# Attention with a gated second branch: the input loaded first, layernorm in groups, and the second branch cut into stages inside the attention loop

**Chip, cores, metric.** One core of a Trainium2 chip. Times are device microseconds (us) of one execution, medians over the runs named. TensorE is PE, VectorE DVE, ScalarE ACT, GpSimd POOL in the profile; L12 is line 12 of the kernel that is spoken of.

## The reference, cut

```python
xn = layernorm(x)                                  # x: 2048 x 640
s  = attention(xn, k_cache, v_cache, wq, wo)       # branch A: 32 heads of 192, last 512 keys
# branch B: a router picks 2 tokens, which get a gated MLP (1536 wide)
r   = xn @ w_r;  idx = argsort(-r)[:2]
y   = (silu(xn[idx] @ w_gate) * (xn[idx] @ w_up)) @ w_down * sigmoid(r[idx])
g   = silu(xn + scatter_add(y at idx))
out = x + s * g
```

Only the last line joins the branches. B's result g is needed at the very end, xn at the very start.

## The kernel before

Attention runs over 16 pairs of heads, four query blocks of 512 rows each: `kT_ps` (keys transposed, once a pair), `q_ps` (query projection), `s_ps` (scores, 8 row tiles a block), softmax on DVE and ACT, `pT_ps` (transposed probabilities), `o_ps`; after each two pairs an output projection (`y_ps`, 192 matmuls) is added into `acc`. A scheduler orders the instructions within each engine; a PE instruction that isn't ready holds up all behind it (here PE stood idle for 9.88 us ahead of the selb matmul of branch B, with attention's work behind it).

```python
loaded = {0: load_pair(0)}                 # 16 loads on the SyncE queue, ahead of x
for t in range(NT):                        # NT = 16 tiles of 128 rows
    eng = nc.sync if t % 2 == 0 else nc.gpsimd
    eng.dma_start(out=x_all[:, t, :], ...)
    ... bn_stats, bn_aggr -> mv_all[:, t]
rstd_all = ...                             # one step for all 16 tiles
for t in range(NT):
    nc.vector.tensor_scalar(out=xn_all[:, t, :], in0=x_all[:, t, :], ...)   # L140
    for d0 in range(0, DT, 4):             # 4 blocks, then 1: two PSUM tiles, two copies
        pst = ps_a.tile(...)               # ps_a has two buffers
        ... nc.tensor.transpose(pst[:, dt, :], ...)                         # L146
        nc.any.tensor_copy(out=xnT[...], in_=pst[...])                      # L147
# branch B in one piece, bs pool with 3 buffers for its weights
r_ps (L162) -> r_row -> r_bf -> r_rt -> max (L170) -> max_index (L172) -> selb -> E
xs_ps (L211, 80 matmuls) -> h: 24 loads w_c, 120 matmuls y_ps (L223) -> down (L241) -> gate g (L249, L251)
... then: for pi in range(NPAIR): attention
```

Of the kernel before, what the change touches and what calls it, by code (L numbers as in the profile page):

```python
# [8 lines left out]
ACT = mybir.ActivationFunctionType  # L9
ALU = mybir.AluOpType  # L10
AX = mybir.AxisListType
F32 = mybir.dt.float32  # L12
BF16 = mybir.dt.bfloat16
# [6 lines left out]
def kernel(  # L20
# [97 lines left out]
    loaded = {0: load_pair(0)}  # L118

    with tc.tile_pool(name="ln", bufs=1) as lnp, tc.tile_pool(name="lns", bufs=4) as lns:  # L120
        FMAX = nc.vector.BN_STATS_FMAX
        nch = (D + FMAX - 1) // FMAX
        while D % nch != 0:
            nch += 1
        csz = D // nch
        x_all = lnp.tile([P, NT, D], BF16, name="x_all")
        mv_all = lnp.tile([P, NT, nc.vector.BN_AGGR_DIM], F32, name="mv_all")
        for t in range(NT):
            eng = nc.sync if t % 2 == 0 else nc.gpsimd
            eng.dma_start(out=x_all[:, t, :], in_=x2[t * P:(t + 1) * P, :])  # L130
            stats = lns.tile([P, nch, nc.vector.BN_STATS_DIM], F32, name="stats")
            for c in range(nch):
                nc.vector.bn_stats(out=stats[:, c, :], in_=x_all[:, t, c * csz:(c + 1) * csz])  # L133
            nc.vector.bn_aggr(out=mv_all[:, t, :], in_=stats[:])
        rstd_all = lnp.tile([P, NT], F32, name="rstd_all")
        nc.vector.tensor_scalar_add(out=rstd_all[:], in0=mv_all[:, :, 1], scalar1=EPS)
        nc.scalar.activation(out=rstd_all[:], in_=rstd_all[:], func=ACT.Sqrt)
        nc.vector.reciprocal(out=rstd_all[:], in_=rstd_all[:])
        for t in range(NT):
            nc.vector.tensor_scalar(out=xn_all[:, t, :], in0=x_all[:, t, :], scalar1=mv_all[:, t, 0:1],  # L140
                                    scalar2=rstd_all[:, t:t + 1], op0=ALU.subtract, op1=ALU.mult)
# [7 lines left out]
    with tc.tile_pool(name="bw", bufs=1) as bw, tc.tile_pool(name="bs", bufs=3) as bs:  # L149
# [3 lines left out]
        wg_v = B_w_gate.rearrange("(dt p) f -> p dt f", p=P)  # L153
        wu_v = B_w_up.rearrange("(dt p) f -> p dt f", p=P)

        r_row = bw.tile([1, S], F32, name="r_row", tag="rowA")
        RC = 512
        for c0 in range(0, S, RC):
# [5 lines left out]
            nc.vector.tensor_copy(out=r_row[:, c0:c0 + cw], in_=r_ps[:, :cw])  # L164
        r_bf = bw.tile([1, S], BF16, name="r_bf")
        nc.vector.tensor_copy(out=r_bf[:], in_=r_row[:])
        r_rt = bw.tile([1, S], F32, name="r_rt", tag="rowB")
        nc.vector.tensor_copy(out=r_rt[:], in_=r_bf[:])
        mx8 = bw.tile([1, 8], F32, name="mx8")
        nc.vector.max(out=mx8[:], in_=r_rt[:])  # L170
        idx8 = bw.tile([1, 8], U32, name="idx8")
        nc.vector.max_index(out=idx8[:], in_max=mx8[:], in_values=r_rt[:])  # L172
        sel = bw.tile([1, 4], F32, name="sel")
        nc.vector.tensor_copy(out=sel[:, 0:2], in_=idx8[:, 0:2])
        nc.vector.tensor_copy(out=sel[:, 2:4], in_=mx8[:, 0:2])
# [10 lines left out]
        sig = bw.tile([2, 1], F32, name="sig")  # L186
        nc.scalar.activation(out=sig[:], in_=selT[:, 1:2], func=ACT.Exp, scale=-1.0)
        nc.vector.tensor_scalar_add(out=sig[:], in0=sig[:], scalar1=1.0)
        nc.vector.reciprocal(out=sig[:], in_=sig[:])

        iota_tok_i = bw.tile([P, NT], I32, name="iota_tok_i")
        nc.gpsimd.iota(iota_tok_i[:], pattern=[[P, NT]], base=0, channel_multiplier=1)
        iota_tok = bw.tile([P, NT], F32, name="iota_tok")
        nc.vector.tensor_copy(out=iota_tok[:], in_=iota_tok_i[:])
        E = bw.tile([P, NT, 2], BF16, name="E")
        for j in range(2):
            nc.vector.tensor_scalar(out=E[:, :, j], in0=iota_tok[:], scalar1=selb[:, j:j + 1],
                                    scalar2=None, op0=ALU.is_equal)
        iota_row_i = bw.tile([2, S], I32, name="iota_row_i", tag="rowA")
        nc.gpsimd.iota(iota_row_i[:], pattern=[[1, S]], base=0, channel_multiplier=0)  # L200
        iota_row = bw.tile([2, S], F32, name="iota_row", tag="rowB")
        nc.vector.tensor_copy(out=iota_row[:], in_=iota_row_i[:])
        ET = bw.tile([2, S], BF16, name="ET")
        nc.vector.tensor_scalar(out=ET[:], in0=iota_row[:], scalar1=selT[:, 0:1], scalar2=0.5,
                                op0=ALU.is_equal, op1=ALU.mult)

        xselT = bw.tile([P, DT, 2], BF16, name="xselT")
        xs_ps = ps_a.tile([P, DT, 2], F32, name="xs_ps", tag="ps_a")
        for dt in range(DT):
            for c in range(NT):  # L210
                nc.tensor.matmul(xs_ps[:, dt, :], lhsT=xn_all[:, c, dt * P:(dt + 1) * P], rhs=E[:, c, :],  # L211
                                 start=(c == 0), stop=(c == NT - 1))
        nc.vector.tensor_copy(out=xselT[:], in_=xs_ps[:])

        h_ps2 = ps_y.tile([P, 2, 512], F32, name="y_ps2")
        hg_ps = h_ps2[:, 0, :2 * FT].rearrange("p (f j) -> p f j", j=2)
        hu_ps = h_ps2[:, 1, :2 * FT].rearrange("p (f j) -> p f j", j=2)
        for (w_v, h_ps, eng) in ((wg_v, hg_ps, nc.gpsimd), (wu_v, hu_ps, nc.gpsimd)):
            for ft in range(FT):
                w_c = bs.tile([P, DT, P], BF16, name="w_c", tag="bs")  # L220
                eng.dma_start(out=w_c[:], in_=w_v[:, :, ft * P:(ft + 1) * P])
# [176 lines left out]
```

## Time and profile before

| | us |
|---|---|
| median of the first 5 runs | 1164.95 (1163.77 to 1170.2) |
| span of the profiled run | 1166.7 |
| PE busy | 1088.5 (93%) |
| first `kT_ps` / first `s_ps` (here and below the second matmul of the first pair; the first starts 0.2 earlier) | 69.7 / 78.4 |

The prediction below shows the totals, the stages and the chain of the head. The pace of the transposes, from the timeline (start, us, instruction, in brackets the idle time before it and who ended it):

```profile
34.08 0.69 PE L146 MATMUL pst<-ident,xn_all 128*128 128x128 bf16 x5 [0.57 <-ACT xnT L147]
34.71 0.75 ACT L147 COPY xnT<-pst 128x512 bf16<-128x512 bf16 x2 [0.51 <-PE pst L146]
35.34 0.69 PE L146 MATMUL pst<-ident,xn_all 128*128 128x128 bf16 x5 [0.57 <-ACT xnT L147]
```

PE and ACT take turns: a tile needs both PSUM buffers, so PE waits for ACT's copies before the next tile, 1.26 us a tile. What B's weight tile w_c made the engines wait for (us, times):

```profile
  DMA w_c<-in_B_w_up_dram: 8.6, 15
  DMA w_c<-in_B_w_gate_dram: 3.7, 9
```

### The profile page before, as it was taken

What the parts mean: (1) busy time and instruction counts of PE and PEld (TensorE: products, weight loads), DVE (VectorE), ACT (ScalarE), POOL (GpSimd) and SP (SyncE); (2) the same over time, 40 slices, a digit from 0 to 9 for tenths busy, and PEclk for the clock granted to TensorE, in tenths of its full rate; (3) what the DMA queues carried; (4) which work ended last, traced back from release to release, by engine and by line L of the source; (5) the groups of instructions that cost most, each with busy time, mean ns of one, the idle gap of its engine ahead of it and who ended that gap; (6) DMA issues with size and microseconds to landing.
All of it is one profiled execution on the core that took longest, in us unless ns stands there. A gap on an engine that the chain in (4) does not pass through costs nothing.

```text
span 1166.7 us, 19485 instructions
## 1 busy us (share of the span) xinstructions
PE 1088.5 (93%) x7178; PEld 589.2 (51%) x7178; DVE 896.9 (77%) x2206; ACT 735.4 (63%) x1701; POOL 52.2 (4%) x85
## 2 busy tenths in 40 slices
PE   0568999999999999999999999999999999999996
PEld 0334445654456545654456445654456545654553
DVE  4567889668966989578966989578966989578995
ACT  0336778457854878458754878468754878468651
POOL 3044000000000000000000000000000000000000
PEclk9979999999999999999999999999999999999997
DMA  9034110111020200112020100112020100010121
GB/s 228 1 76 125 31 32 19 28 35 36 11 45 21 45 14 18 28 35 40 7 45 26 40 15 18 28 35 41 5 44 27 40 15 17 15 35 1 41 63 62
DMA packets 125119, 43.33 MB, mean 37 GB/s; under 512 B 111968, under 2 KB 123232, under 8 KB 125024
## 3 DMA queue, kind: packets, MB, share of 16 engines
q1 hardware_dynamic: 122496, 34.88, 13.5%
q0 software_dynamic: 2528, 7.21, 2.1%
q8 instruction: 56, 0.92, 0.3%
q14 instruction: 39, 0.32, 0.1%
HBM read 39.45 MB, written 2.62 MB: 36 GB/s over the span
## 4 chain that ended last, share of the span: by engine, by line
PE 75%; DVE 9%; ACT 8%; issue 3%; DMA 2%; SPq 1%; POOL 0%; ACTq 0%; POOLq 0%
PE o_ps L345 18%; PE y_ps L269 16%; PE q_ps L310 13%; PE pT_ps L338 9%; PE s_ps L324 9%; PE s_ps L325 7%; ACT p_sb L330 5%; DVE nmx L327 2%; ACT oT_p L347 2%; DVE acc L277 1%; ACT pT L340 1%; DVE stats L133 1%; DMA w_c<-in_B_w_up_dram 1%; DVE diag L335 1%; DMA wd_c<-in_B_w_down_dram 1%
## 5 line engine op out<-in xcount | busy, mean ns | idle before, releaser
L330 ACT ACTIVATE p_sb<-s_ps,nmx 128x512 bf16<-128x512 f32 x512 | 352.1, 690 | 101.4 <-DVE nmx L327 77.0
L327 DVE TENSOR_REDUCE nmx<-s_ps 128x1 f32<-128x512 f32 x512 | 347.4, 684 | 32.7 <-PE s_ps L325 25.1
L310 PE MATMUL q_ps<-xnT,wq_p 128*128 128x512 bf16 x960 | 284.0, 381 | 0.6 <-ACT kT_p L300 0.6
L345 PE MATMUL o_ps<-pT,v_p 128*128 128x512 bf16 x1024 | 263.9, 379 | 3.3 <-ACT oT_p L347 0.7
L269 PE MATMUL y_ps<-wo_p,oT_p 128*128 128x320 bf16 x1536 | 247.8, 302 | 4.6 <-DVE acc L277 3.9
L340 ACT CAST pT<-pT_ps 128x512 bf16<-128x512 f32 x312 | 182.3, 584 | 90.7 <-PE pT_ps L338 87.8
L338 PEld LDWEIGHTS <-p_sb 128*128 128x128 bf16 x2048 | 151.8, 97 | 131.5 <-issue 23.3
L338 PE MATMUL pT_ps<-diag,p_sb 128*128 128x128 bf16 x2048 | 199.9, 219 | 5.8 <-DVE diag L335 4.0
L324 PE MATMUL s_ps<-kT_p,qT_p 128*128 128x512 bf16 x512 | 193.5, 378 | 5.0 <-ACT p_sb L330 1.3
L325 PE MATMUL s_ps<-kT_p,qT_p 128*128 128x512 bf16 x512 | 193.7, 378 | 0.0
L269 PEld LDWEIGHTS <-oT_p 128*128 128x128 bf16 x1536 | 148.9, 99 | 82.7 <-issue 6.4
L277 DVE TENSOR_TENSOR acc<-acc,y_ps 128x640 f32<-128x640 f32 x112 | 91.7, 819 | 107.0 <-PE y_ps L269 106.2
L345 PEld LDWEIGHTS <-v_p 128*128 128x128 bf16 x1024 | 98.2, 97 | 128.0 <-issue 33.5
L347 ACT CAST oT_p<-o_ps 128x512 bf16<-128x512 f32 (+1 forms) x164 | 95.6, 583 | 102.6 <-PE o_ps L345 102.1
L340 DVE CAST pT<-pT_ps 128x512 bf16<-128x512 f32 x200 | 137.8, 689 | 20.6 <-PE pT_ps L338 14.9
L335 DVE TENSOR_SCALAR diag<-ident,rr 128x128 bf16<-128x128 bf16 x512 | 131.7, 257 | 8.0
L310 PEld LDWEIGHTS <-wq_p 128*128 128x128 bf16 x960 | 89.1, 98 | 70.9 <-issue 2.7
L315 ACT ACTIVATE qT_p<-q_ps 128x512 bf16<-128x512 f32 x128 | 76.7, 599 | 53.1 <-PE q_ps L310 53.0
L330 ACT ACTIVATION_READ_ACCUMULATOR p_sb<-s_ps,nmx 128x1 f32 x512 | 102.7, 201 | 0.0
L333 DVE RECIPROCAL rr<-rs 128x1 f32<-128x1 f32 x512 | 80.3, 157 | 25.3 <-ACT p_sb L330 21.1
L325 PEld LDWEIGHTS <-qT_p 128*128 128x128 bf16 x512 | 49.6, 97 | 47.8 <-issue 25.3
L347 DVE CAST oT_p<-o_ps 64x512 bf16<-64x512 f32 (+1 forms) x92 | 63.4, 689 | 11.7 <-PE o_ps L345 11.4
(82 smaller groups left out, 407.5 us busy)
## 6 DMA issues: line engine op xcount, KB each, us to landing
wq_p<-in_A_wq_dram SPq DMA_DIRECT2D x32, 160.0 KB, 2.8
wo_p<-in_A_wo_dram SPq DMA_DIRECT2D x32, 160.0 KB, 2.5
k_p<-in_A_k_cache_dram SPq DMA_DIRECT2D x32, 128.0 KB, 2.4
v_p<-in_A_v_cache_dram SPq DMA_DIRECT2D x32, 128.0 KB, 2.5
wq_p<-in_A_wq_dram SPq DMA_DIRECT2D x32, 80.0 KB, 2.8
wo_p<-in_A_wo_dram SPq DMA_DIRECT2D x32, 80.0 KB, 2.4
x_f<-in_A_x_dram SPq DMA_DIRECT2D x16, 160.0 KB, 2.3
out_dram<-o_t SPq DMA_DIRECT2D x16, 160.0 KB, 1.8
```

Source lines behind the costliest of these rows:

```text
L269: nc.tensor.matmul(y_ps2[:, nh, :NH], lhsT=oT_g[:, b, ts_], rhs=wo_g[:, b, nh * NH:(nh + 1) * NH], start=(i == 0), stop=(i == nmm - 1))
L277: nc.vector.tensor_tensor(out=acc_v, in0=acc_v, in1=y_ps2[:, :, :NH], op=ALU.add)
L310: nc.tensor.matmul(q_ps[:], lhsT=wq_p[:, dt, b, :], rhs=xnT[:, dt, q0:q0 + QC], start=(dt == 0), stop=(dt == DT - 1))
L324: nc.tensor.matmul(s_ps[:], lhsT=qT_p[:, bq, qs], rhs=kT_p[:, 3 * hh, :], start=True, stop=False)
L325: nc.tensor.matmul(s_ps[:], lhsT=qT_p[:, 1, qs], rhs=kT_p[:, 1 + hh, :], start=False, stop=True)
L327: nc.vector.tensor_reduce(out=nmx[:], in_=s_ps[:], axis=AX.X, op=ALU.max, negate=True)
L330: nc.scalar.activation(out=p_sb[:], in_=s_ps[:], func=ACT.Exp, bias=nmx[:], scale=1.0, accum_out=rs[:])
L335: nc.vector.tensor_scalar_mul(out=diag[:], in0=ident[:], scalar1=rr[:])
L338: nc.tensor.matmul(pT_ps[:, kt, :], lhsT=p_sb[:, kt * P:(kt + 1) * P], rhs=diag[:], start=True, stop=True)
L340: nc.any.tensor_copy(out=pT[:, :, qs], in_=pT_ps[:])
L345: nc.tensor.matmul(o_ps[:], lhsT=v_p[:, kt, b, :], rhs=pT[:, kt, :], start=(kt == 0), stop=(kt == KT - 1))
L347: nc.any.tensor_copy(out=oT_p[rows, b, q0:q0 + QC], in_=o_ps[rows, :])
```

## The change

The intent: begin attention as early as possible and let B's work lie inside it. x is loaded first and normalized in place, in four groups of 4 tiles; B becomes functions that run ahead of chosen query blocks, from the ninth on (pair 2), when output projections are there to keep PE busy; its weights get 10 buffers; two row casts and the copy of iota_row go. The diff, cut to its core:

```diff
-    loaded = {0: load_pair(0)}
-        for t in range(NT):  ... load x_all, bn_stats, bn_aggr      # all 16 tiles
-        ... rstd_all
-        for t in range(NT):  ... normalize, transpose
+    for t in range(NT):
+        eng.dma_start(out=xn_all[:, t, :], in_=x2[t * P:(t + 1) * P, :])
+    loaded[0] = load_pair(0)
+    for g in range(NT // LG):            # LG = 4
+        ln_stats(g)
+        ln_norm(g)                       # in place, then the transposes
...
-    with tc.tile_pool(name="bw", bufs=1) as bw, tc.tile_pool(name="bs", bufs=3) as bs:
+    bs = ctx.enter_context(tc.tile_pool(name="bs", bufs=10))
+    stages = [b_stage1, b_stage2, b_stage3, b_stage4, b_stage5]   # router, selection, xs, h, down
+    stages += four stages of the gate, 4 tiles each               # (abridged)
+    for i, st in enumerate(stages):
+        b_sched.setdefault(slots[min(i + 8, len(slots) - 1)], []).append(st)
...
         for qc in range(NQC):
+            for st in b_sched.pop((pi, qc), []):
+                st()
...
-        nc.vector.max(out=mx8[:], in_=r_rt[:])     # after casts r_row -> r_bf -> r_rt
+        nc.vector.max(out=mx8[:], in_=r_bf[:])     # r_bf straight from PSUM
```

More of the change, by code (lines that the diff above doesn't have):

```diff
@@ L116, in load_pair @@
         return wq_p, wo_p, k_p, v_p
-    loaded = {0: load_pair(0)}
-    with tc.tile_pool(name="ln", bufs=1) as lnp, tc.tile_pool(name="lns", bufs=4) as lns:
-        FMAX = nc.vector.BN_STATS_FMAX
-        nch = (D + FMAX - 1) // FMAX
-        while D % nch != 0:
-            nch += 1
-        csz = D // nch
-        x_all = lnp.tile([P, NT, D], BF16, name="x_all")
-        mv_all = lnp.tile([P, NT, nc.vector.BN_AGGR_DIM], F32, name="mv_all")
-        for t in range(NT):
-            eng = nc.sync if t % 2 == 0 else nc.gpsimd
-            eng.dma_start(out=x_all[:, t, :], in_=x2[t * P:(t + 1) * P, :])
+    loaded = {}
@@ new lines, with ln_stats @@
+    FMAX = nc.vector.BN_STATS_FMAX
+    nch = (D + FMAX - 1) // FMAX
+    while D % nch != 0:
+        nch += 1
+    csz = D // nch
+    lns = ctx.enter_context(tc.tile_pool(name="lns", bufs=4))
+    LG = 4
+    for t in range(NT):
+        eng = nc.sync if t % 2 == 0 else nc.gpsimd
+        eng.dma_start(out=xn_all[:, t, :], in_=x2[t * P:(t + 1) * P, :])
+    loaded[0] = load_pair(0)
+    LN = {}
+    def ln_stats(g):
+        mv = lns.tile([P, LG, nc.vector.BN_AGGR_DIM], F32, name="mv")
+        for k in range(LG):
+            t = g * LG + k
@@ L131 @@
             stats = lns.tile([P, nch, nc.vector.BN_STATS_DIM], F32, name="stats")
             for c in range(nch):
-                nc.vector.bn_stats(out=stats[:, c, :], in_=x_all[:, t, c * csz:(c + 1) * csz])
-            nc.vector.bn_aggr(out=mv_all[:, t, :], in_=stats[:])
-        rstd_all = lnp.tile([P, NT], F32, name="rstd_all")
-        nc.vector.tensor_scalar_add(out=rstd_all[:], in0=mv_all[:, :, 1], scalar1=EPS)
-        nc.scalar.activation(out=rstd_all[:], in_=rstd_all[:], func=ACT.Sqrt)
@@ L138 @@
-        nc.vector.reciprocal(out=rstd_all[:], in_=rstd_all[:])
-        for t in range(NT):
-            nc.vector.tensor_scalar(out=xn_all[:, t, :], in0=x_all[:, t, :], scalar1=mv_all[:, t, 0:1],
-                                    scalar2=rstd_all[:, t:t + 1], op0=ALU.subtract, op1=ALU.mult)
+                nc.vector.bn_stats(out=stats[:, c, :], in_=xn_all[:, t, c * csz:(c + 1) * csz])
+            nc.vector.bn_aggr(out=mv[:, k, :], in_=stats[:])
+        rstd = lns.tile([P, LG], F32, name="rstd")
@@ new lines, in ln_stats, with ln_norm @@
+        nc.vector.tensor_scalar_add(out=rstd[:], in0=mv[:, :, 1], scalar1=EPS)
+        nc.scalar.activation(out=rstd[:], in_=rstd[:], func=ACT.Sqrt)
+        nc.vector.reciprocal(out=rstd[:], in_=rstd[:])
+        LN[g] = (mv, rstd)
+    def ln_norm(g):
+        mv, rstd = LN.pop(g)
+        for k in range(LG):
+            t = g * LG + k
+            nc.vector.tensor_scalar(out=xn_all[:, t, :], in0=xn_all[:, t, :], scalar1=mv[:, k, 0:1],
+                                    scalar2=rstd[:, k:k + 1], op0=ALU.subtract, op1=ALU.mult)
@@ L147, with b_stage1 @@
                 nc.any.tensor_copy(out=xnT[:, d0:d0 + dn, t * P:(t + 1) * P], in_=pst[:, :dn, :])
-    with tc.tile_pool(name="bw", bufs=1) as bw, tc.tile_pool(name="bs", bufs=3) as bs:
+    for g in range(NT // LG):
+        ln_stats(g)
+        ln_norm(g)
+    bw = ctx.enter_context(tc.tile_pool(name="bw", bufs=1))
+    bs = ctx.enter_context(tc.tile_pool(name="bs", bufs=10)); bth = ctx.enter_context(tc.tile_pool(name="bth", bufs=2))
+    class _NS:
+        pass
+    B = _NS()
+    wg_v = B_w_gate.rearrange("(dt p) f -> p dt f", p=P)
+    wu_v = B_w_up.rearrange("(dt p) f -> p dt f", p=P)
+    def b_stage1():
         wr_col = bw.tile([P, DT], BF16, name="wr_col")
@@ L152 @@
             nc.gpsimd.dma_start(out=wr_col[:], in_=B_w_r.rearrange("(dt p) -> p dt", p=P))
-        wg_v = B_w_gate.rearrange("(dt p) f -> p dt f", p=P)
-        wu_v = B_w_up.rearrange("(dt p) f -> p dt f", p=P)
-        r_row = bw.tile([1, S], F32, name="r_row", tag="rowA")
+        r_bf = bw.tile([1, S], BF16, name="r_bf")
         RC = 512
@@ L163, with b_stage2 @@
                                  start=(dt == 0), stop=(dt == DT - 1))
-            nc.vector.tensor_copy(out=r_row[:, c0:c0 + cw], in_=r_ps[:, :cw])
-        r_bf = bw.tile([1, S], BF16, name="r_bf")
-        nc.vector.tensor_copy(out=r_bf[:], in_=r_row[:])
-        r_rt = bw.tile([1, S], F32, name="r_rt", tag="rowB")
-        nc.vector.tensor_copy(out=r_rt[:], in_=r_bf[:])
-        mx8 = bw.tile([1, 8], F32, name="mx8")
-        nc.vector.max(out=mx8[:], in_=r_rt[:])
-        idx8 = bw.tile([1, 8], U32, name="idx8")
-        nc.vector.max_index(out=idx8[:], in_max=mx8[:], in_values=r_rt[:])
-        sel = bw.tile([1, 4], F32, name="sel")
-        nc.vector.tensor_copy(out=sel[:, 0:2], in_=idx8[:, 0:2])
-        nc.vector.tensor_copy(out=sel[:, 2:4], in_=mx8[:, 0:2])
+            nc.vector.tensor_copy(out=r_bf[:, c0:c0 + cw], in_=r_ps[:, :cw])
+        mx8 = bw.tile([1, 8], BF16, name="mx8")
+        nc.vector.max(out=mx8[:], in_=r_bf[:])
+        idx8 = bw.tile([1, 8], U32, name="idx8")
+        nc.vector.max_index(out=idx8[:], in_max=mx8[:], in_values=r_bf[:])
+        B.sel = bw.tile([1, 4], F32, name="sel")
+        nc.vector.tensor_copy(out=B.sel[:, 0:2], in_=idx8[:, 0:2])
+        nc.vector.tensor_copy(out=B.sel[:, 2:4], in_=mx8[:, 0:2])
+        iota_tok_i = bw.tile([P, NT], I32, name="iota_tok_i")
+        nc.gpsimd.iota(iota_tok_i[:], pattern=[[P, NT]], base=0, channel_multiplier=1)
+        B.iota_tok = bw.tile([P, NT], F32, name="iota_tok")
+        nc.vector.tensor_copy(out=B.iota_tok[:], in_=iota_tok_i[:])
+    def b_stage2():
+        sel = B.sel
         selb_ps = ps_a.tile([P, 4], F32, name="selb_ps", tag="ps_a")
@@ L185 @@
         nc.vector.tensor_copy(out=selT[:], in_=selT_ps[:])
-        sig = bw.tile([2, 1], F32, name="sig")
-        nc.scalar.activation(out=sig[:], in_=selT[:, 1:2], func=ACT.Exp, scale=-1.0)
-        nc.vector.tensor_scalar_add(out=sig[:], in0=sig[:], scalar1=1.0)
-        nc.vector.reciprocal(out=sig[:], in_=sig[:])
-        iota_tok_i = bw.tile([P, NT], I32, name="iota_tok_i")
-        nc.gpsimd.iota(iota_tok_i[:], pattern=[[P, NT]], base=0, channel_multiplier=1)
-        iota_tok = bw.tile([P, NT], F32, name="iota_tok")
-        nc.vector.tensor_copy(out=iota_tok[:], in_=iota_tok_i[:])
-        E = bw.tile([P, NT, 2], BF16, name="E")
+        B.sig = bw.tile([2, 1], F32, name="sig")
+        nc.scalar.activation(out=B.sig[:], in_=selT[:, 1:2], func=ACT.Exp, scale=-1.0)
+        nc.vector.tensor_scalar_add(out=B.sig[:], in0=B.sig[:], scalar1=1.0)
+        nc.vector.reciprocal(out=B.sig[:], in_=B.sig[:])
+        B.E = bw.tile([P, NT, 2], BF16, name="E")
         for j in range(2):
-            nc.vector.tensor_scalar(out=E[:, :, j], in0=iota_tok[:], scalar1=selb[:, j:j + 1],
+            nc.vector.tensor_scalar(out=B.E[:, :, j], in0=B.iota_tok[:], scalar1=selb[:, j:j + 1],
                                     scalar2=None, op0=ALU.is_equal)
@@ L200, with b_stage3 @@
         nc.gpsimd.iota(iota_row_i[:], pattern=[[1, S]], base=0, channel_multiplier=0)
-        iota_row = bw.tile([2, S], F32, name="iota_row", tag="rowB")
-        nc.vector.tensor_copy(out=iota_row[:], in_=iota_row_i[:])
-        ET = bw.tile([2, S], BF16, name="ET")
-        nc.vector.tensor_scalar(out=ET[:], in0=iota_row[:], scalar1=selT[:, 0:1], scalar2=0.5,
+        B.ET = bw.tile([2, S], BF16, name="ET")
+        nc.vector.tensor_scalar(out=B.ET[:], in0=iota_row_i[:], scalar1=selT[:, 0:1], scalar2=0.5,
                                 op0=ALU.is_equal, op1=ALU.mult)
-        xselT = bw.tile([P, DT, 2], BF16, name="xselT")
+    def b_stage3():
+        B.xselT = bw.tile([P, DT, 2], BF16, name="xselT")
         xs_ps = ps_a.tile([P, DT, 2], F32, name="xs_ps", tag="ps_a")
@@ L210, with b_stage4 @@
             for c in range(NT):
-                nc.tensor.matmul(xs_ps[:, dt, :], lhsT=xn_all[:, c, dt * P:(dt + 1) * P], rhs=E[:, c, :],
+                nc.tensor.matmul(xs_ps[:, dt, :], lhsT=xn_all[:, c, dt * P:(dt + 1) * P], rhs=B.E[:, c, :],
                                  start=(c == 0), stop=(c == NT - 1))
-        nc.vector.tensor_copy(out=xselT[:], in_=xs_ps[:])
+        nc.vector.tensor_copy(out=B.xselT[:], in_=xs_ps[:])
+    def b_stage4():
         h_ps2 = ps_y.tile([P, 2, 512], F32, name="y_ps2")
@@ L217 @@
         hu_ps = h_ps2[:, 1, :2 * FT].rearrange("p (f j) -> p f j", j=2)
-        for (w_v, h_ps, eng) in ((wg_v, hg_ps, nc.gpsimd), (wu_v, hu_ps, nc.gpsimd)):
+        for (w_v, h_ps) in ((wg_v, hg_ps), (wu_v, hu_ps)):
             for ft in range(FT):
                 w_c = bs.tile([P, DT, P], BF16, name="w_c", tag="bs")
-                eng.dma_start(out=w_c[:], in_=w_v[:, :, ft * P:(ft + 1) * P])
+                nc.gpsimd.dma_start(out=w_c[:], in_=w_v[:, :, ft * P:(ft + 1) * P])
                 for dt in range(DT):
-                    nc.tensor.matmul(h_ps[:, ft, :], lhsT=w_c[:, dt, :], rhs=xselT[:, dt, :],
+                    nc.tensor.matmul(h_ps[:, ft, :], lhsT=w_c[:, dt, :], rhs=B.xselT[:, dt, :],
                                      start=(dt == 0), stop=(dt == DT - 1))
         eg = bw.tile([P, FT, 2], F32, name="eg")
-        nc.scalar.activation(out=eg[:], in_=hg_ps[:], func=ACT.Exp, scale=-1.0)
+        nc.scalar.activation(out=eg[:], in_=hg_ps, func=ACT.Exp, scale=-1.0)
         nc.vector.tensor_scalar_add(out=eg[:], in0=eg[:], scalar1=1.0)
@@ L229 @@
         sg = bw.tile([P, FT, 2], F32, name="sg")
-        nc.vector.tensor_tensor(out=sg[:], in0=hg_ps[:], in1=eg[:], op=ALU.mult)
-        guT = bw.tile([P, FT, 2], BF16, name="guT")
-        nc.vector.tensor_tensor(out=guT[:], in0=sg[:], in1=hu_ps[:], op=ALU.mult)
-        y_sb = bw.tile([2, D], BF16, name="y_sb")
-        if True:
-            ps_g = ps_y
-            y_ps = ps_g.tile([P, 2, 512], F32, name="y_ps2")
-            for ft in range(FT):
-                wd_c = bs.tile([P, D], BF16, name="wd_c", tag="bs")
-                nc.gpsimd.dma_start(out=wd_c[:], in_=B_w_down[ft * P:(ft + 1) * P, :])
-                for nh in range(2):
-                    nc.tensor.matmul(y_ps[:2, nh, :NH], lhsT=guT[:, ft, :], rhs=wd_c[:, nh * NH:(nh + 1) * NH],
-                                     start=(ft == 0), stop=(ft == FT - 1))
-            nc.vector.tensor_scalar(out=y_sb[:].rearrange("p (a n) -> p a n", a=2), in0=y_ps[:2, :, :NH],
-                                    scalar1=sig[:, 0:1], scalar2=None, op0=ALU.mult)
-            for c in range(NT):
-                g_ps = ps_g.tile([P, 2, 512], F32, name="y_ps2")
-                for nh in range(2):
-                    nc.tensor.matmul(g_ps[:, nh, :NH], lhsT=ident_h[:], rhs=xn_all[:, c, nh * NH:(nh + 1) * NH],
-                                     start=True, stop=False)
-                    nc.tensor.matmul(g_ps[:, nh, :NH], lhsT=ET[:, c * P:(c + 1) * P], rhs=y_sb[:, nh * NH:(nh + 1) * NH],
-                                     start=False, stop=True)
-                th = bs.tile([P, 2, NH], F32, name="th", tag="bs")
-                nc.scalar.activation(out=th[:], in_=g_ps[:, :, :NH], func=ACT.Tanh)
-                nc.vector.scalar_tensor_tensor(out=xn_all[:, c, :].rearrange("p (a n) -> p a n", a=2),
-                                               in0=th[:], scalar=1.0, in1=g_ps[:, :, :NH],
-                                               op0=ALU.add, op1=ALU.mult)
@@ new lines, in b_stage4, with b_stage5 @@
+        nc.vector.tensor_tensor(out=sg[:], in0=hg_ps, in1=eg[:], op=ALU.mult)
+        B.guT = bw.tile([P, FT, 2], BF16, name="guT")
+        nc.vector.tensor_tensor(out=B.guT[:], in0=sg[:], in1=hu_ps, op=ALU.mult)
+    def b_stage5():
+        B.y_sb = bw.tile([2, D], BF16, name="y_sb")
+        y_ps = ps_y.tile([P, 2, 512], F32, name="y_ps2")
+        for ft in range(FT):
+            wd_c = bs.tile([P, D], BF16, name="wd_c", tag="bs")
+            nc.gpsimd.dma_start(out=wd_c[:], in_=B_w_down[ft * P:(ft + 1) * P, :])
+            for nh in range(2):
+                nc.tensor.matmul(y_ps[:2, nh, :NH], lhsT=B.guT[:, ft, :], rhs=wd_c[:, nh * NH:(nh + 1) * NH],
+                                 start=(ft == 0), stop=(ft == FT - 1))
+        nc.vector.tensor_scalar(out=B.y_sb[:].rearrange("p (a n) -> p a n", a=2), in0=y_ps[:2, :, :NH],
+                                scalar1=B.sig[:, 0:1], scalar2=None, op0=ALU.mult)
@@ new lines, in b_stage_g @@
+    def b_stage_g(c):
+        g_ps = ps_y.tile([P, 2, 512], F32, name="y_ps2")
+        for nh in range(2):
+            nc.tensor.matmul(g_ps[:, nh, :NH], lhsT=ident_h[:], rhs=xn_all[:, c, nh * NH:(nh + 1) * NH],
+                             start=True, stop=False)
+            nc.tensor.matmul(g_ps[:, nh, :NH], lhsT=B.ET[:, c * P:(c + 1) * P], rhs=B.y_sb[:, nh * NH:(nh + 1) * NH],
+                             start=False, stop=True)
+        th = bth.tile([P, 2, NH], F32, name="th")
+        nc.scalar.activation(out=th[:], in_=g_ps[:, :, :NH], func=ACT.Tanh)
+        nc.vector.scalar_tensor_tensor(out=xn_all[:, c, :].rearrange("p (a n) -> p a n", a=2),
+                                       in0=th[:], scalar=1.0, in1=g_ps[:, :, :NH],
+                                       op0=ALU.add, op1=ALU.mult)
@@ L258 @@
+    b_sched = {}
+    slots = [(pi_, qc_) for pi_ in range(NPAIR) for qc_ in range(NQC)]
+    stages = [b_stage1, b_stage2, b_stage3, b_stage4, b_stage5]
+    GPS = 4
+    for c0 in range(0, NT, GPS):
+        stages.append(lambda c0=c0: [b_stage_g(c) for c in range(c0, min(NT, c0 + GPS))])
+    for i, st in enumerate(stages):
+        b_sched.setdefault(slots[min(i + 8, len(slots) - 1)], []).append(st)
     g_all = xn_all
@@ L357 @@
                 group = []
-    with tc.tile_pool(name="fin", bufs=3) as fin:
-        for t in range(NT):
-            x_t = fin.tile([P, D], BF16, name="x_f")
-            nc.sync.dma_start(out=x_t[:], in_=x2[t * P:(t + 1) * P, :])
-            tmp = fin.tile([P, D], F32, name="tmp")
-            nc.vector.tensor_tensor(out=tmp[:], in0=acc[:, t, :], in1=g_all[:, t, :], op=ALU.mult)
-            o_t = fin.tile([P, D], BF16, name="o_t")
-            nc.vector.tensor_tensor(out=o_t[:], in0=tmp[:], in1=x_t[:], op=ALU.add)
-            nc.sync.dma_start(out=out2[t * P:(t + 1) * P, :], in_=o_t[:])
+    for key in sorted(b_sched):
+        for st in b_sched[key]:
+            st()
+    for t in range(NT):
+        x_t = bs.tile([P, D], BF16, name="x_f", tag="bs")
+        nc.sync.dma_start(out=x_t[:], in_=x2[t * P:(t + 1) * P, :])
+        nc.vector.tensor_tensor(out=acc[:, t, :], in0=acc[:, t, :], in1=g_all[:, t, :], op=ALU.mult)
+        o_t = bs.tile([P, D], BF16, name="o_t", tag="bs")
+        nc.vector.tensor_tensor(out=o_t[:], in0=acc[:, t, :], in1=x_t[:], op=ALU.add)
+        nc.sync.dma_start(out=out2[t * P:(t + 1) * P, :], in_=o_t[:])
 _INS = ['A_x', 'A_k_cache', 'A_v_cache', 'A_wq', 'A_wo', 'B_x', 'B_w_r', 'B_w_gate', 'B_w_up', 'B_w_down']
```

## The prediction

> **What bounds the kernel now.** I read the page's totals first, then the 40 slices, then a table of busy time by stage, then the chain that ended last inside the first 130 us.
>
> ```profile
> PE 1088.5 (93%) x7178; PEld 589.2 (51%) x7178; DVE 896.9 (77%) x2206; ACT 735.4 (63%) x1701; POOL 52.2 (4%) x85
> ...
> PE   0568999999999999999999999999999999999996
> ...
> PEclk9979999999999999999999999999999999999997
> ```
>
> TensorE (PE) is busy 93% of 1166.7 us, so it is idle for only 78 us, and the slices put most of that in the first four of 40 (29 us each). The same four slices hold the only low clock but for the last one. The stage table (columns: stage, its length, then busy us and instructions of PE, weight load, DVE, ACT, POOL; then granted clock, DMA share, GB/s) says how much:
>
> ```profile
> 0.00:33.00 33.00, 0.20 (x3) 0.20 (x4) 15.45 (x54) 1.50 (x2) 9.71 (x21) 1.00 0.85 202
> 33.00:70.00 37.00, 19.91 (x189) 13.25 (x188) 22.50 (x47) 11.53 (x22) 2.86 (x3) 0.86 0.01 0
> 70.00:120.00 50.00, 45.71 (x359) 21.29 (x357) 32.11 (x85) 28.49 (x66) 24.80 (x33) 0.93 0.43 118
> 120.00:1120.00 1000.00, 989.26 (x6450) 536.85 (x6448) 794.51 (x1964) 679.02 (x1581) 14.83 (x28) 1.00 0.13 28
> 1120.00:1167.00 47.00, 33.45 (x188) 17.65 (x185) 32.34 (x60) 14.83 (x33) 0.00 (x0) 0.84 0.20 63
> ```
>
> PE's idle time, length minus busy, is 32.8, 17.1, 4.3, 10.7 and 13.6 us. The middle 1000 us has 1% idle: nothing to win there, and anything added to PE there is paid in full. The head has 54 us. Why it is idle, the chain of waits tells (start, us, what):
>
> ```profile
> 13.02 4.47 DMA x_all<-in_A_x_dram
> 17.52 1.28 DVE stats L133 x3
> ...
> 32.30 5.80 DVE xn_all L140 x16
> ...
> 50.24 5.81 PE r_ps L162 x20
> 56.07 0.69 DVE r_row L164
> 56.79 1.23 DVE r_bf L166
> 58.03 2.95 DVE r_rt L168
> 61.01 2.29 DVE mx L170
> 63.32 2.35 DVE idx L172 x2
> ...
> 67.53 2.27 PE xs_ps L211 x80
> 69.80 0.34 PE kT_ps L293 x3
> ```
>
> The input x is the last thing the SyncE queue issues (13 us, behind the 16 loads of pair 0); the layernorm statistics of all 16 tiles must end before the first normalization (32.3); the transposes end at 50; then branch B's router runs matmul, five serial one-partition DVE instructions and 80 matmuls with no attention beside it. Attention starts at 69.8.
>
> **What the Trainium skill says.** "TensorE: Matmul & The Clock Gate", Part 1, says that the array's clock halves after an idle window of about 3.4 us. The trace agrees after work had begun: 9.88 us of PE idle before the selb matmul, and the granted clock is 0.50 from 65.9 to 69.8. It does not agree for the idle first 33 us, recorded as 1.00. The same page, Part 2, step 1, says that matmuls stay in program order and only weight loads are pulled ahead: a B matmul placed inside attention that isn't ready holds all attention behind it. The trace shows that already: the h matmuls (L223) were waited for by DMA for 8.6 + 3.7 us in total on the weights' queue. "ScalarE: Activation LUTs", What ACT_TABLE_LOAD costs, gives 1283 ns; the trace has 1.28 us at 67.2. The changed code keeps Sqrt before all Exp and Tanh, and the built order of ACT shows two loads as before, so nothing is added there. "DMA: Bandwidth & Descriptors", Anatomy of one DMA, gives about 2 us fixed per transfer; here 160 KB weights land in 2.4 to 2.8 us in the steady part.
>
> **The change, part by part.**
> 1. x first, normalized in place, in four groups of 4 tiles. Eight x tiles head the SyncE queue and eight the GpSimd queue. The first issue is at 0.75 us instead of 13.0, so the first statistics come at about 4 us. One tile's statistics pace at 0.86 us (0.75 + 0.11 in the chain), one normalization at 0.36 (5.80/16). The built DVE order puts the first normalization behind the statistics of seven tiles: 4 + 7 x 0.86 + about 0.5 for rstd = 10.5 us. The transposes then cost 1.26 us a tile as long as ACT does both copies (34.08, 35.34, 36.60 are the starts before) and 1.0 later: about 19.5 us for 16, so until 30 to 31. DVE's own sum, 16 x 0.86 + 5.8 + 2 for the small ones = 21.6, ends at 25.6, and four tiles' transposes from 24.5 end at about 30: the same. Pair 0's loads now follow x: 24 issues of 0.5 to 0.75 us end at 17, landing by about 21, in time. Attention starts at 31 instead of 69.8: gain 38.7 us.
> 2. The wait for weights. Ten buffers instead of three for w_c and wd_c, ten loads issued long ahead. The 4.3 us of idle in 70 to 120 and the low clock there (clock 0.89 over 69.8 to 102.3 loses about 3 us of work) go: gain 7.3 us.
> 3. Router and selection on PE move into the full stretch: 20 r_ps in 5.8 us and 80 xs_ps in 2.3 us: loss 8.1 us. The h, down and gate matmuls shared PE with attention before too: no difference.
> 4. DVE's serial work moves into pair 2: four row copies of 0.68, MAX8 2.28, FIND_INDEX8 2.27, ET 1.27, together 8.5 us, while PE needs DVE every 12 matmuls to empty the single y_ps buffer (copy 0.825). The built PE order puts 36 y_ps, 15 q_ps and 4 s_ps, some 9 us, between the last r_ps and the selb matmul, against about 6 us of chain, so selb itself is ready; but each long instruction can hold up one y_ps copy. I charge half: loss 4 us. Two row casts (1.23 + 2.95) and iota_row are gone, which was head time, already counted in part 1.
> 5. The last 14 w_c loads are issued only as h matmuls free buffers, 0.87 us each on GpSimd: 12.2 us, for matmuls that the PE order spreads over about 12.6 us. Loss 2 us.
> 6. The end: x_f has more buffers and the product goes in place in acc. The last chain is y_ps, acc, tmp, o_t (3.4 + 3 x 0.83 us) in both: 0.
>
> Sum: 38.7 + 7.3 - 8.1 - 4 - 2 = 31.9 us. 1164.95 - 31.9 = 1133 us.
>
> **The rivals.**
> First, B is not additive but hidden. From 260 to 320 us, without wo_project, DVE is busy 53.26 of 60, and 37 s_ps pairs pass, so a block of 8 takes 13 us, while its matmuls at 0.216 us a 512-column one need about 12. The first eight blocks after the change are of this kind, with nothing else for PE, and B's matmuls could lie in the slack of the blocks in pairs 3 and 4. Then parts 3 to 5 cost almost nothing: about 1120. Against it: PE is 99% busy in that stretch already.
> Second, the chain of B takes the place of the wait: PE, in order, stands at selb, xs_ps or h because DVE or GpSimd lags behind the order that the scheduler assumed. GpSimd has the memsets of kT_p for pairs 2 and 3 ahead of the last 14 w_c loads, and the first x_f load sits in the SyncE queue ahead of v_p of pair 4 until wd_c buffers are free. If each of five stages costs 3 us more than I charge: 1148.
> Third, the first group's in-place layernorm waits for x: 16 loads at once, landing in 5.2 us median before, share the engines with pair 0. If attention starts at 38 instead of 31: 1140.
>
> **Range and chances.** The head gain is the surest part (plus or minus 5); the charge for B inside attention is the weakest (0 to 25 instead of 14). Predicted 1133 us, 1120 to 1146 in 8 of 10. The 2% line is 1141.7, some 9 us above the prediction: faster 0.78, within 2% 0.20, slower 0.02.
>
> **What would show it.** In the profile after: the first kT_ps near 31 us, first s_ps soon behind; PE idle before 120 us near 20 instead of 54; no stretch at clock 0.5 before the end; the router's matmuls with little idle ahead of them, selb waiting under 2 us for DVE; DVE acc waits of PE a few us more; w_c waits near 2. The prediction is wrong if the first kT_ps comes after 40, if idle by B's lines passes 15 us, or if the blocks of pairs 0 and 1 take much more than 13 us each.

## The result, and the profile after

1132.3 us (median of 8 runs, 1130.1 to 1136.3) against 1165.05 (15 runs of before beside it): ratio 0.9712, 95% interval 0.9695 to 0.9729. Ratios are the mean time of one kernel's fast runs over that of the other's of the same rounds, so not quite the ratio of the medians. Four more runs, 1130.0 to 1139.3, are not in that count; the median of all 12 is 1133.1. The gain is 2.9%, faster by over 2%.

The page after, totals and slices:

```profile
PE 1085.7 (96%) x7178; PEld 588.6 (52%) x7178; DVE 879.2 (78%) x2183; ACT 746.4 (66%) x1730; POOL 52.2 (5%) x85
...
PE   3999999999999999999999999999999999999995
```

PE's idle time fell from 78.2 to 47.1 us (span minus busy), 31.1 us, and its busy time by 2.8; the sum is the span's 33.9. The stages of the kernel after (columns as in the prediction's table):

```profile
0.00:31.00 31.00, 10.51 (x76) 7.87 (x77) 22.78 (x79) 12.38 (x31) 18.64 (x31) 1.00 1.04 228
31.00:37.00 6.00, 5.01 (x24) 2.76 (x24) 1.07 (x3) 2.34 (x5) 0.00 (x0) 1.00 0.87 183
37.00:120.00 83.00, 81.45 (x498) 40.46 (x497) 70.89 (x185) 65.48 (x156) 1.07 (x2) 1.00 0.09 17
120.00:1087.00 967.00, 956.07 (x6395) 520.02 (x6394) 753.30 (x1860) 650.51 (x1508) 32.49 (x52) 1.00 0.14 31
1087.00:1133.00 46.00, 32.64 (x189) 17.50 (x188) 31.11 (x58) 15.72 (x35) 0.00 (x0) 0.88 0.23 72
```

The head to 120 us is idle for 23.0 us instead of 54.2; the middle (10.9) and the last 46 us (13.4) are as before. The chain through the head:

```profile
1.30 3.92 DMA xn_all<-in_A_x_dram
5.24 0.49 DVE stats L140
...
11.25 1.76 DVE xn_all L152 x4
...
16.72 0.60 PE pst L158 x4
17.34 0.59 ACT xnT L159
17.98 0.60 PE pst L158 x4
...
31.95 1.03 PE kT_ps L323 x8
...
34.22 6.14 PE q_ps L342 x15
40.36 0.22 PE s_ps L356
```

The x tile that the chain waits for lands at 5.2 instead of 17.5, the first normalization starts at 11.3 instead of 32.3, and the transposes, paced by the turns of PE and ACT (16.72, 17.98), end, with their copies, at 31.9 instead of 50. No router chain follows.

For all kernels below, milestones counted in the traces. "P1 last" is the last `y_ps` of the first output projection, "P3 first" the first of the third, behind all of B in every kernel; these are used since the y_ps records are complete in all traces, which the s_ps records are not.

| kernel | first kT_ps | first s_ps | P1 last | P3 first | span | median us |
|---|---|---|---|---|---|---|
| before | 69.7 | 78.4 | 245.1 | 403.0 | 1166.7 | 1165.05 |
| after | 32.0 | 40.4 | 187.2 | 369.8 | 1132.8 | 1132.3 |
| x first alone | 57.5 | 66.4 | 234.9 | 392.8 | 1152.7 | 1154.1 |
| part 1 alone | 51.7 | 60.2 | 227.4 | 385.3 | 1148.5 | 1151.1 |
| B moved alone | 48.5 | 56.0 | 202.5 | 385.4 | 1144.7 | 1148.7 |
| after without B | 32.2 | 40.1 | 183.9 | 341.2 | 1104.0 | 1103.9 |
| 3 weight buffers | 31.8 | 38.8 | 185.6 | 370.6 | 1134.6 | 1139.5 |
| short router | 33.2 | 40.8 | 186.7 | 370.7 | 1129.7 | 1131.6 |
| B from block 1 | 32.1 | 44.7 | 212.6 | 371.9 | 1130.8 | 1133.2 |
| layernorm interleaved | 12.2 | 32.5 | 189.5 | 371.9 | 1130.9 | 1135.5 |
| after again | 33.3 | 41.7 | 188.4 | 371.1 | 1131.8 | 1132.9 |
| one copy | 27.3 | 35.4 | 181.8 | 364.5 | 1125.3 | 1126.9 |
| queries early | 14.4 | 27.6 | 177.9 | 360.3 | 1119.8 | 1122.4 |

Read it so: at P1 the changed kernel is 57.9 us ahead, because attention started 38 earlier and B did not slow the first pairs; at P3, once B is paid, 33.2; the end keeps that. In the round of runs 1 to 4 the kernel before was slower than elsewhere (median 1168.9, clock mostly 0.986), which flatters their ratios a little; for them the P3 column is the better measure.

### The profile page after: what moved, and what is told of

It reads as the page before. It is cut to its first block, busy times and chain, and to the rows that moved or that the text cites.

```text
span 1132.8 us, 19452 instructions
## 1 busy us (share of the span) xinstructions
PE 1085.7 (96%) x7178; PEld 588.6 (52%) x7178; DVE 879.2 (78%) x2183; ACT 746.4 (66%) x1730; POOL 52.2 (5%) x85
## 3 DMA queue, kind: packets, MB, share of 16 engines
q1 hardware_dynamic: 122496, 34.88, 14.1%
## 4 chain that ended last, share of the span: by engine, by line
PE 78%; ACT 11%; DVE 8%; issue 3%; DMA 0%; ACTq 0%; POOL 0%; DVEq 0%; POOLq 0%
PE o_ps L377 19%; PE y_ps L299 16%; PE q_ps L342 14%; PE pT_ps L370 9%; PE s_ps L356 9%; PE s_ps L357 7%; ACT p_sb L362 6%; DVE nmx L359 3%; ACT pT L372 2%; ACT oT_p L379 1%; DVE diag L367 1%; DVE acc L307 1%; ACT qT_p L347 1%; PE kT_ps L323 1%; PE pst L158 1%
## 5 line engine op out<-in xcount | busy, mean ns | idle before, releaser
L359 DVE TENSOR_REDUCE nmx<-s_ps 128x1 f32<-128x512 f32 x512 | 347.6, 684 | 31.8 <-PE s_ps L357 25.0
L299 PE MATMUL y_ps<-wo_p,oT_p 128*128 128x320 bf16 x1536 | 244.0, 301 | 4.7 <-DVE acc L307 3.6
L372 ACT CAST pT<-pT_ps 128x512 bf16<-128x512 f32 x307 | 179.1, 583 | 81.1 <-PE pT_ps L370 77.3
L379 ACT CAST oT_p<-o_ps 128x512 bf16<-128x512 f32 (+1 forms) x188 | 109.3, 581 | 128.3 <-PE o_ps L377 127.4
L372 DVE CAST pT<-pT_ps 128x512 bf16<-128x512 f32 x205 | 141.1, 688 | 21.7 <-PE pT_ps L370 17.0
L367 DVE TENSOR_SCALAR diag<-ident,rr 128x128 bf16<-128x128 bf16 x512 | 129.1, 253 | 8.2
L365 DVE RECIPROCAL rr<-rs 128x1 f32<-128x1 f32 x512 | 80.1, 157 | 31.2 <-ACT p_sb L362 25.5
L357 PEld LDWEIGHTS <-qT_p 128*128 128x128 bf16 x512 | 49.6, 97 | 49.4 <-issue 30.0
L356 PEld LDWEIGHTS <-qT_p 128*128 128x128 bf16 x512 | 50.0, 98 | 24.1 <-issue 1.2
```

Of the source, the lines that this page charges most:

```text
L299: nc.tensor.matmul(y_ps2[:, nh, :NH], lhsT=oT_g[:, b, ts_], rhs=wo_g[:, b, nh * NH:(nh + 1) * NH], start=(i == 0), stop=(i == nmm - 1))
L356: nc.tensor.matmul(s_ps[:], lhsT=qT_p[:, bq, qs], rhs=kT_p[:, 3 * hh, :], start=True, stop=False)
L357: nc.tensor.matmul(s_ps[:], lhsT=qT_p[:, 1, qs], rhs=kT_p[:, 1 + hh, :], start=False, stop=True)
L359: nc.vector.tensor_reduce(out=nmx[:], in_=s_ps[:], axis=AX.X, op=ALU.max, negate=True)
L367: nc.vector.tensor_scalar_mul(out=diag[:], in0=ident[:], scalar1=rr[:])
L372: nc.any.tensor_copy(out=pT[:, :, qs], in_=pT_ps[:])
```

## The experiments

Each started from one of the two kernels; the outputs passed the comparison with the reference in all. That says little where B is cut or spoiled: the comparison did not notice. Presumably s * g is small beside x; nobody measured it.

**1. x first alone.** The kernel before, loads reordered.

```diff
-    loaded = {0: load_pair(0)}
+    ... the 16 loads of x ...
+    loaded[0] = load_pair(0)
```

> The kernel before with one change: the 16 loads of x are issued ahead of the 16 loads of pair 0. Theory (the head is one serial chain from x to the first kT_ps, and nothing of it but the load moves): statistics start near 5.2 us as in the changed kernel instead of 17.5, first kT_ps near 57.5 instead of 69.7, time 12.3 us less, 1153 us. Rival (pair 0's loads, now later, take the place of x as the wait, or the shared engines slow x down): first kT_ps after 63, gain under 6 us, 1159 or more.

1154.1 us, ratio 0.9872 (0.9838 to 0.9906); first kT_ps at 57.5, as written. The head is one serial chain from x's landing; the later loads of pair 0 took its place nowhere. Of the 12.2 us won there, 10.2 are left at P3.

**2. Part 1 alone.** The kernel before with x first and layernorm in groups; B in one piece.

```diff
-    all statistics, one rstd step, all normalizations
+    for g in range(NT // LG):
+        ln_stats(g)
+        ln_norm(g)
```

> The kernel before with part 1 of the change alone: x first, layernorm in four groups, in place; branch B stays in one piece ahead of attention. Theory: transposes end near 32 us, the router's chain then takes its 19.7 us as before, first kT_ps near 51.6 instead of 69.7, gain 18 us, 1147 us. Rival (grouping overlaps with B's chain only when B moves, so part 1 alone is worth no more than x first): 1153.

First kT_ps at 51.7, as written; 1151.1 us (1145.3 to 1152.5), ratio 0.9843 (0.98 to 0.9886). The gain in the trace is 18.2 us (spans 1166.7 and 1148.5). The median lies 4 us above what was written; the interval holds it. The one run at a clock of 0.994 took 1145.3, the three at 0.986 to 0.988 took 1150.4 to 1152.5. At P3 the gain is 17.7.

**3. B moved alone.** The changed kernel with the old head.

```diff
+    loaded = {0: load_pair(0)}          # ahead of x again
-        ln_stats(g)
-        ln_norm(g)
+    all ln_stats, then all ln_norm
```

> The changed kernel with the old head: pair 0's loads first, statistics of all 16 tiles before the first normalization; branch B stays cut into stages inside attention. Theory: transposes end near 50 us, first kT_ps near 50 instead of 69.7, B's matmuls paid in attention; gain of about 19.7 - 4 = 16 us, 1149 us, and with the gain of part 1 alone the two add up to the whole 33. Rival (moving B is worth nothing by itself since it is paid in full elsewhere): under 6 us gain, 1159 or more.

1148.7 us, ratio 0.9834 (0.9804 to 0.9863). Attention starts 21.2 us earlier (48.5), 17.6 are left at P3. Parts 1 and B alone gain 1.6% and 1.7%, together 3.2% against 2.9% for the whole: additive within the intervals. At P3 it is 17.7 and 17.6, together 35.3, against 33.2. Each of runs 1 to 3 alone stays within 2%; only the whole gains more.

**4. After without B.** Wrong on purpose: g is xn.

```diff
-    for i, st in enumerate(stages):
+    for i, st in enumerate([]):
```

> The changed kernel with all stages of branch B left out (wrong result on purpose: g is the normalized x). Theory (B is additive on TensorE: the 128 s_ps after the 64th come 29 us late after the change against two steady periods of 131 us): time 29 us less than the changed kernel, 1103 us; the period from the 64th to the 128th s_ps shrinks from 157 to about 131. Rival (B lies in the slack of the DVE-bound blocks): 1120 or more.

1103.9 us, 28.4 less than the changed kernel. The stretch from the 64th to the 128th s_ps, in the order before, after, after without B (each its own trace; length, then busy us and instructions of PE, weight load, DVE, ACT, POOL):

```profile
203.00:333.10 130.10, 128.59 (x836) 69.66 (x835) 101.25 (x256) 88.16 (x207) 2.08 (x4) 1.00 0.14 28
```

```profile
139.50:296.20 156.70, 155.63 (x1155) 83.12 (x1154) 118.14 (x290) 99.91 (x228) 20.67 (x30) 1.00 0.22 55
```

```profile
139.00:270.00 131.00, 129.31 (x849) 70.66 (x849) 101.63 (x257) 89.65 (x210) 2.18 (x4) 1.00 0.13 28
```

The changed kernel needs 156.7 us where the two others need 130 to 131, and PE is busy for 99% in all: B costs PE time one for one. The first rival of the prediction, B hidden in slack, falls.

**5. Three weight buffers.** The changed kernel.

```diff
-    bs = ctx.enter_context(tc.tile_pool(name="bs", bufs=10))
+    bs = ctx.enter_context(tc.tile_pool(name="bs", bufs=3))
```

> The changed kernel with 3 buffers for B's weights instead of 10 (x_f and o_t at the end share them). Theory of the prediction (the waits for weights before, 12.3 us in total by the h matmuls' line, come from the three buffers; ten of them hide the loads): the h matmuls (120, now in 18 us) wait for DMA again, the loads come in threes at some 3 us a round, 21 loads in 7 rounds, of which PE's attention work hides a part: 8 to 15 us slower than the changed kernel, 1140 to 1147. Rival (attention work between the h matmuls hides any load, the scheduler places them later): within 2 us of 1132.

1139.5 us (1136.4 to 1141.1), ratio 0.9779 (0.9765 to 0.9793) against 0.9712 and 0.9734 for the changed kernel: about 0.5 to 0.7% slower, by medians 7 us, just under what was written. In its trace the h matmuls (L243) wait again:

```profile
  DMA w_c<-in_B_w_up_dram: 11.5, 14
  DMA w_c<-in_B_w_gate_dram: 2.4, 6
```

Of these 13.9 us the matmuls' own idle time is 4.2. With ten buffers that list is empty, and the 120 matmuls pass in 18 us instead of 34. But the profiled run, the fastest of its four, lost only 1.8 us by its span (2.4 us between P1 and P3, 185.0 against 182.6); where the slower runs lost the rest, no trace shows. The edit also leaves x_f and o_t at the end with 3 buffers, a rival that no run separates.

**6. Short router.** The changed kernel; wrong selection on purpose.

```diff
-        nc.vector.max(out=mx8[:], in_=r_bf[:])
-        nc.vector.max_index(out=idx8[:], in_max=mx8[:], in_values=r_bf[:])
+        nc.vector.max(out=mx8[:], in_=r_bf[:, :8])
+        nc.vector.max_index(out=idx8[:], in_max=mx8[:], in_values=r_bf[:, :8])
```

> The changed kernel with MAX8 and FIND_INDEX8 over 8 elements instead of 2048 (wrong selection on purpose), which takes 2 x 2.2 us of serial DVE work out of pair 2. Prediction's charge (each long DVE instruction holds up one y_ps copy, half of it paid): 2 us less, 1130. Rival (PE has work enough beside them, no wait for DVE of B shows in the trace after): no difference, 1132.3 within 0.7.

1131.6 us, ratio 0.9724 (0.9701 to 0.9747): no difference that the interval can tell, though it is too wide to exclude 2 us. The edit cut MAX8 and FIND_INDEX8 from 2.28 and 2.27 us to 0.16 and 0.15, about half of the 8.5 us that were charged for. What settles the charge is what y_ps waited for, which the pages list last in its line, here for the changed kernel and for the one without B:

```profile
L299 PE MATMUL y_ps<-wo_p,oT_p 128*128 128x320 bf16 x1536 | 244.0, 301 | 4.7 <-DVE acc L307 3.6
L299 PE MATMUL y_ps<-wo_p,oT_p 128*128 128x320 bf16 x1536 | 244.7, 301 | 4.5 <-DVE acc L307 3.6
```

3.6 us with B and without it (3.9 in the kernel before): B's serial DVE work held up next to no y_ps copy. PE had y_ps, q_ps and s_ps to run beside it, and the selb matmul did not wait.

**7. B from the first block on.** The changed kernel.

```diff
-        b_sched.setdefault(slots[min(i + 8, len(slots) - 1)], []).append(st)
+        b_sched.setdefault(slots[min(i + 0, len(slots) - 1)], []).append(st)
```

> The changed kernel with B's stages placed from the first query block of pair 0 on instead of from the ninth. If B is simply additive on TensorE: the same time, 1132 within 3. If the blocks of pairs 0 and 1, which have no output projection and leave PE about 1 us of slack each, hide a part of B: 5 to 10 us less, 1122 to 1127. If the router's serial chain, the selection and the weights' loads stall PE there, since no output projection is there to run meanwhile: 5 us or more slower, 1137 or more.

1133.2 us, ratio 0.9723 (0.9709 to 0.9737): the same. The place matters little for the sum. It does for one wait: ahead of the selb matmul PE now stands idle until DVE's router chain ends. Those who waited for DVE's sel (us, times):

```profile
  PEld selb_ps L202: 2.9, 1
  PE selb_ps L202: 2.4, 1
```

Weight load and matmul wait side by side, so this is one wait of 2.4 us of PE; in the changed kernel the selb matmul doesn't wait. At P3 this kernel is 0.8 and 2.1 us behind the two traces of the changed one, so the wait may just be paid, below what the medians can tell.

**8. Layernorm interleaved, meant to be better.** PE still idles 20.5 of the first 31 us, because the order on PE puts all 16 tiles' transposes ahead of kT_ps.

```diff
-    for g in range(NT // LG):
-        ln_stats(g)
-        ln_norm(g)
...
         for qc in range(NQC):
+            if pi == 0:
+                ln_stats(qc)
+                ln_norm(qc)
```

> A version meant to be better: the changed kernel, with each layernorm group's statistics, normalization and transposes placed in pair 0's query block that needs it, so that the first q_ps waits for 4 tiles instead of 16. Theory (in the first 32 us PE still idles 20 us, as it waits for all 16 tiles although the first query block needs 4): first s_ps near 25 us instead of 40.4, but DVE has 10 us of layernorm still to do beside the first blocks, which run at DVE's pace: 5 to 10 us less, 1122 to 1127. Rival (DVE bounds both layernorm and the first blocks, so the start only looks earlier): 1132 within 3.

1135.5 us, ratio 0.9743 (0.9729 to 0.9757), by medians 2.6 to 3.2 us above the changed kernel, with an interval that overlaps that of its repeat: the gain of 5 to 10 us did not come. Attention started 8 us earlier (32.5), and at P1 it is 2.3 us behind (1.1 behind the repeat of run 9). Two lines of its chain and one of its stages:

```profile
15.37 5.88 DMA k_p<-in_A_k_cache_dram
21.30 0.62 PE kT_ps L319 x4
...
32.00:120.00 88.00, 79.78 (x523) 41.32 (x532) 78.30 (x224) 71.24 (x163) 1.08 (x2) 1.00 0.13 27
```

kT_ps now comes first on PE and waits for k, whose last piece is issued behind the v, wq and wo of the other blocks; the transposes of x wait behind it, in order. And from 32 to 120 DVE, with the rest of layernorm beside the softmax of the first blocks, is busy for 78.3 us; the changed kernel has 71.7 there. (PE's columns can't be compared: 456 of the 512 second s_ps matmuls have a record in this trace.) From the first s_ps to P1 this kernel takes 157.0 us, the changed one 146.8. Two things are in these 10.2 us: the 60 transposes of three groups, 6.2 us of PE busy time (ends modelled) that the changed kernel spends before attention, and waits of PE for DVE and ACT, 4.0 and 3.5 us against 0.5 each. How much each costs is not separated by a run of its own (the 4.0 and 3.5 may also be off, as records are missing).

**9 to 11. The changed kernel again, and two versions meant to be better.** They ran together on one chip. One copy:

```diff
-        eng = nc.sync if t % 2 == 0 else nc.gpsimd
+        eng = nc.sync if t % 2 == 0 else nc.scalar
-            for d0 in range(0, DT, 4):
-                dn = min(4, DT - d0)
-                pst = ps_a.tile([P, 4, P], BF16, ...)
+            for d0 in range(0, DT, DT):
+                dn = DT
+                pst = ps_a.tile([P, DT, P], BF16, ...)
```

Queries early, on top of it: pair 0's loads in the order k, wq, v, wo, and

```diff
-    for g in range(NT // LG):
-        ln_stats(g)
-        ln_norm(g)
+    ln_stats(0)
+    ln_norm(0)
+    for g in range(1, NT // LG):
+        ln_stats(g)
...
             (after q_ps of a block)
+            if pi == 0 and qc == 0:
+                for g in range(1, NT // LG):
+                    ln_norm(g)
```

> The changed kernel once more, unaltered, as the measure for the two beside it on the same chip: 1132.3 within 2, ratio 0.971 to the kernel before.

> The changed kernel with two edits in its head: the five transposes of a tile go to one PSUM tile and one copy (two copies and two buffers made the pace of 1.26 us a tile), and x's odd tiles are issued by ScalarE's queue instead of GpSimd's (DVE's first statistics waited until 5.2 us for a GpSimd load). Theory (the pace of the transposes, one tile in flight at a time, ends the head at 32): first kT_ps at 28 to 29 instead of 32, set by DVE then; 1129. Rival (DVE's layernorm alone sets the end, copies were hidden): no change, 1132.

> A version meant to be better: the two edits of the one-copy run, and pair 0's k and wq loads ahead of v and wo, and the first query block's kT_ps and q_ps placed behind the first layernorm group, the other groups' normalization and transposes behind those. Unlike in the interleaved version that lost 3 us, no layernorm is left beside later blocks and PE does not wait for k ahead of the transposes. Theory (PE idles 20 of the first 32 us for work that needs 4 tiles only; kT_ps and q_ps are 8.4 us on the path after the last transpose, 6.1 of them for 15 q_ps at half pace): first s_ps near 31 instead of 40.4, 64th s_ps and the end 6 to 9 us earlier, 1123 to 1126. Rival (the first blocks run at DVE's pace and DVE's layernorm sum ends at 27 in any case): 1129 as with the one-copy edits alone.

The changed kernel repeated: 1132.9 us, 0.9734 (0.9704 to 0.9763). One copy: 1126.9 us, 0.9685 (0.9649 to 0.9721); first kT_ps at 27.3, even earlier than written. The last normalizations, the last transposes and the first kT_ps, from the timeline:

```profile
23.80 1.51 DVE L152 TENSOR_SCALAR xn_all<-xn_all,mv,rstd 128x640 bf16<-128x640 bf16 x4
25.80 1.23 PE L158 MATMUL pst<-ident,xn_all 128*128 128x128 bf16 x10 [0.25 <-ACT xnT L159]
27.27 1.69 PE L323 MATMUL kT_ps<-ident,k_p 128*128 128x128 bf16 x12 [0.25 <-DMA k_p<-in_A_k_cache_dram]
```

DVE now sets the end of the head, as written: it is busy for 21.3 of the 23 us from 4 to 27, and the transposes run until 0.25 us before kT_ps. The chain of the profile names a load of k there, but the one it names was issued at 24.57 us and belongs to pair 1 (the 16 loads of pair 0 were all issued by 24.5), so k is not what is waited for. Queries early: 1122.4 us (1121.6 to 1129.5), 0.9652 (0.9619 to 0.9684), the best here, 0.9% below the changed kernel. Its chain:

```profile
17.16 0.60 PE kT_ps L329 x4
...
21.94 5.30 PE q_ps L348 x15
27.25 0.28 PE pst L163 x5
27.52 0.22 PE s_ps L365
```

The 15 q_ps still take 5.3 us, but while DVE normalizes the other groups (22.3 to 27.3). The first s_ps is 14.1 us ahead of its neighbour's (41.7), 10.5 are left at P1 and 10.8 at P3: 3.6 us are given back. From the first s_ps on, PE does 55 of the other groups' 60 transposes (4.5 us busy), while its waits for DVE are 1.0 us against 0.5: the transposes are paid beside attention, as B is.

## Why the prediction was right, by its steps

Predicted 1133.0, measured 1132.3. The mechanism held: attention started as early as written, and B was then paid beside it. That the sum came within 1 us is in part luck, since errors of opposite sign cancelled: two charges, 6 us together, were not there, and the charge for the router was some 1.5 too high, while the 3 us for the low clock were not won and the start was 1 us later.

| term | predicted | measured |
|---|---|---|
| 1. earlier start | +38.7 | +37.7 (first kT_ps 69.7 to 32.0) |
| 2 to 5. B inside attention, net | -6.8 | -3.9 |
| sum | 31.9 | 33.9 by spans, 32.7 by medians |

- **Step 1** held: x first gave 12.2 us (run 1), grouping another 5.8 (run 2), leaving B's chain out of the head the rest (run 3). The first tile's statistics ran at 3.0 us, but the second tile, on GpSimd's queue, landed only at 5.2; about 4 was predicted. Pair 0's issues ended at 19.2 instead of 17, still in time.
- **Steps 2 to 5, net.** From the first to the 64th s_ps the kernel before took 124.6 us, the one after 99.1: 25.5 won. From the 64th to the 192nd it took 260.9 before and 290.3 after: 29.4 paid. Run 4 shows that this payment is B itself: without B the two stretches take 99.1 and 261.9.
- **Step 2, the 3 us for the low clock, was wrong.** From the first kT_ps to the first s_ps it took 8.7 us before and takes 8.4 after: attention starts at half pace in both. In the kernel after, q_ps follow each other every 0.427 us until 39.8 us and every 0.216 from there; the first 15 took 6.14 us, 2.9 more than at full pace, although PE had done transposes since 12 us and was busy for 10.5 of the first 31. The trace's first clock record (full) stands at that same 39.8, in the kernel before at 52.9. The view's 1.00 ahead of it is time without a record, so the prediction's reading "recorded as 1.00" for the first 33 us, as a sign against the half clock, was wrong too.
- **Step 2, the wait for weights**, 4.3 us: the sign for it, 8.6 + 3.7 us, was a sum of weight loads and matmuls; PE's own part was 2.7 before and 0 after.
- **Step 3** charged the 20 r_ps with the 5.8 us that they took in the head, partly at half pace (before 52.9 us). At 0.216 each, an estimate, they cost 4.3 beside attention. With this, and without the charges and the clock term that failed, the net is 4.3 - 6.6 = -2.3, some 2 us from the measured -3.9.
- **Step 4, the DVE charge of 4 us, was wrong**: y_ps waited for acc 3.6 us with B and without it (lines at run 6). PE had the y_ps of the first projection to run. The prediction had counted 9 us of such work against 6 and then charged half of it all the same.
- **Step 5, the refill charge of 2 us, was wrong**: the h matmuls of the changed kernel wait for no DMA. Run 5 shows that the buffers are what keeps them from it.
- **The rivals.** B hidden: fell (run 4). A new chain of waits for B: fell in the changed kernel; run 7 shows a wait of 2.4 us where no projection runs beside it. A late x: kT_ps came at 32, not 38.
- **Step 6** held: PE is idle for 13.6 us of the last 47 before and for 13.4 of the last 46 after. Their granted clock varies between runs of one kernel too (0.88 and 0.94 for the changed kernel), and with it the end.

## What to carry to other kernels

Ask of each idle microsecond of the bounding engine what it waited for, and follow that back to the first load: here 12 us were the order of two groups of loads. Work taken off an idle head and put beside a saturated engine is paid there at its full busy time, so count the gain as idle time removed, not as work moved. An early start is worth only the idle time that it removes: run 8 started 8 us earlier and gained nothing, as its transposes and its waits came after the start in place of before. And read who waits: a wait of a weight load and its matmul is one wait, and a chain may name a load that came last but was not the one needed.

## What the Trainium skill lacked or had wrong

- "TensorE: Matmul & The Clock Gate", Part 1: its gaps between matmuls of 512 columns, 426.7 ns cold and 215.7 warm, are what the first q_ps show (0.427, then 0.216 us). What it doesn't spell out is that a trace may have no clock record ahead of the first change, here at 39.8 us, and that a view which counts such time as full speed prints 1.00 over matmuls at half pace.
- "VectorE: DVE Perf Modes" gives no time for MAX8 and FIND_INDEX8: 2048 elements on one partition took 2282 and 2273 ns, the same for bf16 (after) as for f32 (before); 8 elements took 157 and 148 (run 6).
- No page that I read gives the cost of a step that needs both buffers of a PSUM pool: PE and ACT took turns at 1.26 us a tile, and one PSUM tile and one copy a tile was part of a gain of 6 us (run 10).
